# A planner's margin for VectorE and the first group with shared clusters, in a fused retention and MLP kernel

## The chip, the cores and the metric

The kernel runs on one core of one Trainium2 chip. The metric is the device time of one execution in microseconds (us); the time before is the median of 3 runs.

## The reference

For 8 batches and 8 heads, 576 positions of 64 elements, retention is computed: scores of q and k, scaled by 1/8, times a lower triangular decay of each head, times v. The result, laid out as 4608 tokens of 512 elements, goes through two dense layers with a squared ReLU between them.

```python
scores = scale * np.matmul(q, k.transpose(0, 1, 3, 2))
gamma = 1.0 - 2.0 ** (-5.0 - np.arange(H, dtype=np.float32))
Dmat = np.where(rel >= 0, gamma[:, None, None] ** rel[None, :, :], 0.0)
attn_out = np.matmul(scores * Dmat[None, :, :, :], v)
x = attn_out.transpose(0, 2, 1, 3).reshape(B * S, H * D)
h = x @ w_in                      # 512 -> 2048
r = np.maximum(h, 0.0)
return ((r * r) @ w_out)          # 2048 -> 512
```

## The kernel before

**Units and groups.** The tokens are cut into 36 units of 128 tokens: four full ones per batch, and one "tail" for each pair of batches. Two units make a group; there are 18 groups, 0 to 17, and the program works through them in order.

**Retention.** It is done in chunks with a running state. In each unit, TensorE makes scores (tile `psc`), sums of k and v for the state (`psS`), and outputs (`psO`), all as matmuls on 64x64 quarters of the array, issued by the helper `quad` (L343). VectorE masks the scores (`rT`, or `rx` in groups 0 to 3), updates the states (`stmp`, `Rm`, `R`) and multiplies the outputs by the decay into `xT`. Groups 0 to 3 come from paired loads (`pair`), with transposes on TensorE (`psT`); later units are loaded with `k`, `q`, `v`, cast on GpSimd (`kq`, `v`) and transposed by DMA (`kqT`).

**Clusters.** From group 4 on the matmuls of retention are issued in clusters. A group on its own has two: `fa` (scores and sums) and `fb` (outputs that read older states, a drain of TensorE, and the other outputs). From group `JOIN` on two neighbours share: `f1` is the first outputs of group g with the scores of g + 1, `f2` the sums of g + 1 with the remaining outputs of g. `add_ret` builds them.

**The dense layers.** `add_ff` cuts the 2048 hidden elements into 16 blocks of 128. A block of the first layer is 4 matmuls into a PSUM tile `ph` (L827; two blocks share one tile), followed by a ReLU on ScalarE (`rl`, L835) and a square on ScalarE or VectorE (`gT`). In groups 0 and 1 the second layer is 16 matmuls per unit into `po` (L865). From group 2 on it is a Strassen scheme of seven products (L916) that read `gT`, sums `gS` made by VectorE (L893), and differences `wT` of the weights. PSUM has four tiles for `ph`, `po` and their like.

**The weights** come in eight pieces of 1 MB, here called w0 to w3 (`wi`, of w_in, four hidden blocks each) and w4 to w7 (`wo`, of w_out). GpSimd and ScalarE each cast one half of a piece to 16 bit (L322). Loads, transposes and stores are issued by SyncE in one queue; a load waits for a free staging buffer. Until there is other work TensorE runs filler matmuls (`warm`, L247), 40 of them.

**What sets the order.** Only the first loads are listed by hand. Each piece of work is added to a `Schedule` with an engine, a priority key, a planned duration, what it depends on and which buffers it takes. `emit` plays the plan through once, when the program is built: whenever an engine is free it takes the ready item of lowest key. The instructions are then written out for each engine in the order in which they started in that plan. The chip follows this order whatever the real durations are; semaphores only make it wait. A result becomes ready for a user on another engine `LAT` microseconds after the end of its producer in the plan; buffers are released after the same time:

```python
push(now + (0.0 if w["eng"] == t["eng"] else t["lat"]), "dep", w)
```

Of the kernel before, what the change touches and what calls it, by code (L numbers as in the profile page):

```python
# [14 lines left out]

class Schedule:

    LAT = {"PE": 0.25, "ACT": 0.12, "DVE": 0.12, "POOL": 0.12, "SP": 2.1}

    def __init__(self, count):  # L20
        self.count = dict(count)
# [2 lines left out]
    def add(self, eng, key, dur, fn, deps=(), acq=(), after=None, lag=0.0):  # L24
        t = dict(eng=eng, key=key, dur=dur, fn=fn, acq=acq, n=len(self.tasks), users=[], free=[], lag=lag,
                 left=len(deps), ready=0.0, lat=self.LAT[eng] if after is None else after)
        for d in deps:
# [14 lines left out]
    def emit(self):  # L42
        ready = {e: [] for e in self.LAT}
        busy = {e: False for e in self.LAT}
        events = []
# [58 lines left out]
def kernel(  # L104
# [122 lines left out]
    SQ_ACT = (0, 1, 2, 3, 4, 5, 6)  # L227
    SPREAD = 0.1
    SQ_LATE = (1, 4, 6)
    JOIN = 7  # L230
    LAG = {"v2": 1.2, "w1": 1.3, "k4": 0.7, "q4": 0.5}
    LAG_T, LAG_O = 1.5, 5.0
    PAIRED = 8
# [115 lines left out]
    def add_unit(u, base):  # L349

        kind, b, c = units[u]
        tail = [tail_dec] if kind == "tail" else []

        def sorted_cast(op, out_, in_):
            op(out=out_.rearrange("p (n b a d) -> p n b a d", n=2, b=2, a=2),  # L355
               in_=in_.rearrange("p (n a b) d -> p n b a d", n=2, a=2))

        def fk():
            t = tile_of["kq", u] = cast.tile([P, 2, H * D], FP16, name="kq16", tag="kq16")
            sorted_cast(nc.gpsimd.tensor_copy, t[:, 0], tile_of["k32", u])  # L360

        def fq():
            sorted_cast(nc.gpsimd.tensor_copy, tile_of["kq", u][:, 1], tile_of["q32", u])

        def fv():
            t = tile_of["v16", u] = cast.tile([P, H, D], FP16, name="v16", tag="v16")
            nc.gpsimd.tensor_tensor(  # L367
                out=t, in0=tile_of["v32", u],
                in1=vdec[kind].rearrange("p (h o) -> p h o", o=1).to_broadcast([P, H, D]), op=ALU.mult)
        ck = add("POOL", base, 0.65, fk, deps=[loaded["k", u]], acq=("kq",))  # L370
        cq = add("POOL", base + 1, 0.62, fq, deps=[loaded["q", u], ck])
        cv = add("POOL", base + 2, 1.1, fv, deps=[loaded["v", u]] + tail, acq=("v16",))
        for what, t in (("k", ck), ("v", cv)):
            for w in gate.get((what, u), []):
                sched.need(w, t)
        T["casts", u] = [ck, cq, cv]
        sched.free("ld", [ck, cq, cv])
        def fx2():
            t = tile_of["kqT", u] = work.tile([P, 2 * NP, P], FP16, name="kqT", tag="kqT", bufs=6)
            nc.sync.dma_start_transpose(out=t, in_=tile_of["kq", u].rearrange("p x n -> p (x n)"))  # L380
        T["kqT", u] = [add("SP", -1, 2.7, fx2, deps=[ck, cq], acq=("kqT",), after=3.0, lag=LAG_T)]
# [162 lines left out]
    def units_of(g):  # L544
        return sorted(groups[g])
# [4 lines left out]
    def base_of(g):  # L550
        return (units_of(g)[0] - len(groups[g])) * L - EARLY
# [74 lines left out]
    def joined(g):  # L626

        return JOIN <= g < last_g

# [82 lines left out]
    def add_casts(g):  # L712
        for u in units_of(g):
            if u < PAIRED:
                if u % 2 == 0:
                    add_unit_pair(u, base_of(g) - 5)
                continue
            add_unit(u, base_of(g) - L * (2 if g > JOIN else 1) + 4 * (u - units_of(g)[0]))

# [336 lines left out]
```

## Time and profile before

| what | value |
| --- | --- |
| median of 3 runs | 292.76 us (292.64 to 292.85) |
| the profiled execution | 292.64 us |
| its span, first to last instruction | 290.9 us |
| TensorE busy | 283.0 us, 97% of the span |
| VectorE busy | 195.0 us, 67% |
| ScalarE busy | 187.5 us, 64% |
| GpSimd busy | 88.9 us, 31% |
| HBM, mean over the span | 159 GB/s |

Engines are named in the profile as PE (TensorE matmul), PEld (its weight load), DVE (VectorE), ACT (ScalarE), POOL (GpSimd) and SP (SyncE); a q behind the name is its sequencer. A line of the timeline has start and length in us, engine, line of the kernel, operation, output tile and inputs, shapes and count; brackets hold the idle time of the engine before it and what ended that. A line of the waits has the waiting instruction, what it waited for, us in total, times and the longest. A busy TensorE is not a TensorE at its peak, and the ends of its matmuls are modelled, so starts are compared.

### The profile page before, as it was taken

Reading aid. Unit: us, or ns where it says so; the run is one execution under the profiler, and the core shown is the slowest. Engines: PE = TensorE matmul, PEld = TensorE weight load, DVE = VectorE, ACT = ScalarE, POOL = GpSimd, SP = SyncE. Lnnn points to the kernel's source line nnn. Section 1 sums busy time; section 2 is a strip of 40 time slices with the busy share of each in tenths; the row PEclk is TensorE's granted clock in tenths of the full one; section 3 lists DMA queues with packets and bytes.
Section 4 is the critical chain, followed back from the end, with each engine's and each line's share of the span. In section 5 each row is a group of like instructions: output and inputs, shape, how many; then the busy total and the mean of one; then the engine's idle time right before and its main releaser. Section 6 shows DMA issues by size and latency. Waiting matters only on the chain.

```text
span 290.9 us, 10062 instructions
## 1 busy us (share of the span) xinstructions
PE 283.0 (97%) x4328; PEld 234.0 (80%) x4328; DVE 195.0 (67%) x430; ACT 187.5 (64%) x354; POOL 88.9 (31%) x123
## 2 busy tenths in 40 slices
PE   7989999999999999999999999999999999999994
PEld 2557765688888888888888888888888888888883
DVE  3796589748485848656868857667786865565632
ACT  6456966296757575867666666766767676747830
POOL 5343454524434234251616041615151400000000
PEclk9999999999999999999999999999999999999999
DMA  7999999999999899997998599979896820201004
GB/s 201 327 368 387 370 276 250 239 220 186 233 214 214 185 148 247 221 186 189 196 208 180 126 192 211 202 183 180 211 188 171 159 74 2 74 3 72 2 2 144
DMA packets 139421, 54.13 MB, mean 186 GB/s; under 512 B 118129, under 2 KB 130929, under 8 KB 139377
## 3 DMA queue, kind: packets, MB, share of 16 engines
q1 hardware_dynamic: 139072, 53.23, 81.9%
q8 instruction: 34, 0.56, 0.9%
q10 hardware_dynamic: 304, 0.26, 0.3%
q14 instruction: 11, 0.08, 0.1%
HBM read 36.70 MB, written 9.44 MB: 159 GB/s over the span
## 4 chain that ended last, share of the span: by engine, by line
PE 89%; DMA 6%; SPq 1%; issue 1%; POOL 1%; DVE 0%; DVEq 0%; POOLq 0%
PE ph L827 42%; PE po L916 34%; PE po L865 5%; PE psO L343 4%; DMA wi<-in_moe_w_in_dram 3%; DMA pair<-in_q_dram 3%; PE psc L343 2%; PE psS L343 2%; SPq L298 1%; POOL w_in L322 1%; PE psT L418 1%; DVE o L939 0%; POOL qx L403 0%; DVE p L968 0%; DVEq L939 0%
## 5 line engine op out<-in xcount | busy, mean ns | idle before, releaser
L827 PE MATMUL ph<-xT,w_in 128*128 128x256 f16 x1152 | 139.4, 273 | 0.2 <-POOL w_in L322 0.2
L827 PEld LDWEIGHTS <-w_in 128*128 128x128 f16 x1152 | 111.1, 98 | 14.8 <-POOL w_in L322 0.4
L835 ACT ACTIVATE rl<-ph 128x512 f16<-128x512 f32 x144 | 84.3, 589 | 46.9 <-PE ph L827 45.0
L845 ACT ACTIVATE gT<-rl 128x512 f16<-128x512 f16 x104 | 65.6, 631 | 3.0
L916 PEld LDWEIGHTS <-gS 128*128 128x128 f16 x512 | 49.4, 98 | 6.1 <-DVE gS L893 0.2
L916 PE MATMUL po<-wT,gS 128*128 128x256 f16 x384 | 52.4, 273 | 0.0
L893 DVE TENSOR_TENSOR gS<-gT,gS 128x512 f16<-128x512 f16 x64 | 35.1, 554 | 11.6 <-ACT gT L845 11.0
L916 PEld LDWEIGHTS <-gT 128*128 128x128 f16 x384 | 37.2, 98 | 4.4
L893 DVE TENSOR_TENSOR gS<-gT 128x512 f16<-128x512 f16 x64 | 30.7, 481 | 12.9 <-ACT gT L845 12.9
L916 PE MATMUL po<-w_out,gT 128*128 128x256 f16 x256 | 34.5, 273 | 0.0
L355 POOL CAST kq<-q 128x512 f16<-128x512 f32 x28 | 18.8, 673 | 45.7 <-DMA q<-in_q_dram 45.5
L367 POOL TENSOR_TENSOR v<-v,vdec_full 128x512 f16<-128x512 f32 x24 | 26.2, 1093 | 19.6 <-DMA v<-in_v_dram 14.4
L355 POOL CAST kq<-k 128x512 f16<-128x512 f32 x28 | 18.6, 666 | 44.4 <-DMA k<-in_k_dram 41.7
L847 DVE TENSOR_TENSOR gT<-rl 128x512 f16<-128x512 f16 x40 | 18.9, 473 | 14.7 <-ACT rl L835 14.2
L929 ACT COPY u<-po 128x256 f32<-128x256 f32 x32 | 11.8, 369 | 20.4 <-PE po L916 20.4
L939 DVE TENSOR_TENSOR o<-po,u 128x256 f32<-128x256 f32 x31 | 13.0, 421 | 16.2 <-PE po L916 8.3
L704 DVE TENSOR_TENSOR xT<-psO,gam_full 128x512 f16<-128x512 f32 x28 | 18.9, 686 | 7.5 <-PE psO L343 7.4
L643 DVE TENSOR_TENSOR rT<-psc,mask 128x512 f16<-128x512 f32 x28 | 18.3, 683 | 5.5 <-PE psc L343 5.2
L916 PE MATMUL po<-w_out,gS 128*128 128x256 f16 x128 | 17.0, 273 | 0.0
L916 PE MATMUL po<-wT,gT 128*128 128x256 f16 x128 | 16.8, 273 | 0.0
L939 DVE TENSOR_TENSOR o<-po,p 128x256 f32<-128x256 f32 x17 | 7.2, 424 | 13.7 <-ACT u L929 7.1
L865 PE MATMUL po<-w_out,gT 128*128 128x512 f16 x64 | 15.8, 380 | 0.0
(81 smaller groups left out, 244.1 us busy)
## 6 DMA issues: line engine op xcount, KB each, us to landing
out_dram<-o SPq DMA_DIRECT2D x31, 256.0 KB, 3.0
k<-in_k_dram SPq DMA_DIRECT2D x24, 256.0 KB, 4.5
q<-in_q_dram SPq DMA_DIRECT2D x24, 256.0 KB, 4.8
v<-in_v_dram SPq DMA_DIRECT2D x24, 256.0 KB, 5.3
wi<-in_moe_w_in_dram SPq DMA_DIRECT2D x4, 1024.0 KB, 10.1
wo<-in_moe_w_out_dram SPq DMA_DIRECT2D x4, 1024.0 KB, 9.7
pair<-in_k_dram SPq DMA_DIRECT2D x4, 512.0 KB, 7.0
pair<-in_q_dram SPq DMA_DIRECT2D x4, 512.0 KB, 7.0
```

The source lines that it names most:

```text
L343: nc.tensor.matmul(out_, lhsT=lhsT, rhs=rhs, start=start, stop=True, skip_group_check=True, tile_position=(64 * row, 64 * col))
L355: op(out=out_.rearrange("p (n b a d) -> p n b a d", n=2, b=2, a=2), in_=in_.rearrange("p (n a b) d -> p n b a d", n=2, a=2))
L367: nc.gpsimd.tensor_tensor(out=t, in0=tile_of["v32", u], in1=vdec[kind].rearrange("p (h o) -> p h o", o=1).to_broadcast([P, H, D]), op=ALU. ...
L704: nc.vector.tensor_tensor(out=tile_of["x", g][:, :, s * P:(s + 1) * P].rearrange("p n (c i) -> p c n i", c=2), in0=tile_of["psO", g][:, :, ...
L827: nc.tensor.matmul(tile_of["ph", g, fb][:, j, :], lhsT=w_in16[:, m, fi * P:(fi + 1) * P], rhs=tile_of["x", g][:, m, :], start=(m == 0), st ...
L835: nc.scalar.activation(out=t, in_=tile_of["ph", g, fb], func=ACTF.Relu)
L845: nc.scalar.activation(out=t, in_=rl, func=ACTF.Square)
L847: nc.vector.tensor_tensor(out=t, in0=rl, in1=rl, op=ALU.mult)
L865: nc.tensor.matmul(tile_of["po", u], lhsT=tile_of["g", g][:, fi, s * P:(s + 1) * P], rhs=w_out16[:, fi, :], start=(fi == 0), stop=(fi == N ...
L893: nc.vector.tensor_tensor(out=Sx(k, h), in0=in0(h), in1=in1(h), op=op)
L916: nc.tensor.matmul(tile_of["pb", g, bank], lhsT=left(i), rhs=right[:, i, :], start=(start and i == 0), stop=(i == HF - 1), skip_group_chec ...
L939: nc.vector.tensor_tensor(out=o_tile(u)[:, half * HM:(half + 1) * HM], in0=bank(x), in1=tile_of[name, g], op=ALU.add)
```

## The change

Two constants differ. The time that the plan lets pass until a result of VectorE counts as there on another engine goes from 0.12 to 0.3 us, and the first group with shared clusters from 7 to 8.

```diff
-    LAT = {"PE": 0.25, "ACT": 0.12, "DVE": 0.12, "POOL": 0.12, "SP": 2.1}
+    LAT = {"PE": 0.25, "ACT": 0.12, "DVE": 0.3, "POOL": 0.12, "SP": 2.1}
...
-    JOIN = 7
+    JOIN = 8
```

`JOIN` is read in two places: in `joined`, which tells whether a group shares, and in `add_casts`, where the casts of groups behind it get an earlier key.

```python
return JOIN <= g < last_g
...
add_unit(u, base_of(g) - L * (2 if g > JOIN else 1) + 4 * (u - units_of(g)[0]))
```

The instructions are the same in number and kind; what differs is their order. The order of GpSimd is unchanged. On TensorE, VectorE, ScalarE and SyncE items trade places throughout. On TensorE, group 7's `f1` and `f2` become its `fb` and group 8's `fa`. At the start of TensorE's order these lines move (a block is one first-layer block of the group named):

```diff
 group 0, blocks 1 to 4
-fillers, psO of group 1
 group 0, block 5
+psO of group 1
 group 0, blocks 6 to 12
-group 1, block 1
 group 0, blocks 13 to 16
-group 1, blocks 2 to 4
+group 1, block 1
 group 0, po 1 to 4 of the first unit
...
 group 0, po 13 to 16 of the first unit, all of the second unit
+group 1, blocks 15 and 16
 group 1, po
```

On ScalarE the casts of w3 to w7 each move ahead of one ReLU. On VectorE, at the start, the cast of v for the first pair moves ahead of a copy of `kqT`.

## The prediction

> **What bounds the kernel now.** I read the page first: busy shares, then the chain that ended last.
>
> ```profile
> PE 283.0 (97%) x4328; PEld 234.0 (80%) x4328; DVE 195.0 (67%) x430; ACT 187.5 (64%) x354; POOL 88.9 (31%) x123
> ...
> PEclk9999999999999999999999999999999999999999
> ...
> PE 89%; DMA 6%; SPq 1%; issue 1%; POOL 1%; DVE 0%; DVEq 0%; POOLq 0%
> ```
>
> TensorE has work for 97% of the span at full granted clock, and the chain is TensorE nearly throughout; VectorE, whose planning figure is changed, has a third of its time free. A busy share can hide waits, so next the waits of TensorE:
>
> ```profile
> PE warm L247 <- DVE junk L163: 1.3, 1, 1.3
> PE psO L343 <- DVE R L489: 0.9, 1, 0.9
> PE psT L418 <- DVE qx L403: 0.4, 1, 0.4
> PE psS L343 <- DVE vx L399: 0.3, 1, 0.3
> PE ph L827 <- POOL w_in L322: 0.2, 1, 0.2
> ```
>
> That is all. So I laid out the timeline of TensorE and of GpSimd around those waits:
>
> ```profile
> 20.02 1.04 PE L247 MATMUL warm<-junk 128*128 128x512 f16 x4
> 22.00 0.31 PE L343 MATMUL psO<-kqT,R 64*64 64x128 f16 x8 [0.94 <-DVE R L489]
> ...
> 23.09 4.10 PE L827 MATMUL ph<-xT,w_in 128*128 128x256 f16 x36
> 27.35 0.83 PE L827 MATMUL ph<-xT,w_in 128*128 128x256 f16 x6 [0.15 <-POOL w_in L322]
> ```
>
> ```profile
> 26.25 1.04 POOL L322 CAST w_in<-wi 128x1024 f16<-128x1024 f32 x1 [1.66 <-DMA wi<-in_moe_w_in_dram]
> 28.95 1.04 POOL L322 CAST w_out<-wo 128x1024 f16<-128x1024 f32 x1 [1.66 <-DMA wo<-in_moe_w_out_dram]
> 31.65 1.15 POOL L322 CAST w_out<-wo 128x1024 f16<-128x1024 f32 x1 [1.66 <-DMA wo<-in_moe_w_out_dram]
> 34.32 1.04 POOL L322 CAST w_out<-wo 128x1024 f16<-128x1024 f32 x1 [1.52 <-DMA wo<-in_moe_w_out_dram]
> 37.10 1.29 POOL L322 CAST w_out<-wo 128x1024 f16<-128x1024 f32 x1 [1.74 <-DMA wo<-in_moe_w_out_dram]
> ```
>
> Two regimes. Up to 38.45 the eight 1 MB weight pieces (w0 to w3 of w_in, w4 to w7 of w_out) are cast as they land, every 2.7 us, and TensorE can only fill the time between with what needs no later piece. After 38.45 TensorE never waits as much as 0.1 us: comparing starts of successive matmuls, I find only about 0.09 at each step into a cluster of 64x64 matmuls and 0.05 once near 228. What the start leaves undone at 38.45, and what TensorE's work costs after it, therefore sets the end one for one.
>
> Prices: a first-layer block (4 matmuls of ph) starts 0.437 after the last (16 in 33.89 to 35.63 = 1.74); a second-layer matmul of groups 0 and 1 (po, L865) 0.216.
>
> **Part 1, VectorE's margin 0.12 to 0.3: the start.** The planner holds work that reads VectorE's results back by 0.18, and the orders of TensorE, VectorE, ScalarE and SyncE shift; GpSimd's does not. I walk TensorE's new order.
>
> Before w1 (cast ends 20.63 + 1.04 = 21.67) the changes cost nothing: group 0's chain runs some 0.5 later on VectorE and the fillers (warm) stand elsewhere, but all of it still ends before w1, which the next block needs. If that cover went, the 0.5 would show, but then the next pin, w3, is still ahead.
>
> At w1: before, TensorE waits for R until 22.00, runs psO of group 1 (1.09), then blocks. After, block 5 of group 0 goes first (about 21.7 to 22.2), then psO to 23.3, then blocks 6 to 12: 7 x 0.437 = 3.06, to 26.4 (block 9 may add 0.1 for w2). Block 13 needs w3: 26.25 + 1.04, start 27.35 as before. In the old order block 1 of group 1 stood ahead of it (the ninth of the 36 matmuls at 23.09); in the new one it stands behind. TensorE idles some 0.95 where it idled 0.3.
>
> From 27.35: blocks 13 to 16 and one of group 1, 5 x 0.437 = 2.18, to 29.53. Then the first po, which needs w4: 28.95 + 1.04 + 0.06 (the lag of w3's cast to its matmul) = 30.05, idle 0.5. In the old order three more blocks stood there and nothing idled. Then 4 po 0.86, 6 blocks 2.62 (33.53, w5 at 32.8 is there), 4 po, 3 blocks 1.31 (35.71, w6 at 35.36 is there), 4 po, 4 blocks 1.75: 38.32. The next po needs w7, 37.10 + 1.29 + 0.06 = 38.45, where it starts in the old run too:
>
> ```profile
> 36.50 1.91 PE L827 MATMUL ph<-xT,w_in 128*128 128x256 f16 x16
> 38.45 1.89 PE L865 MATMUL po<-w_out,gT 128*128 128x512 f16 x8
> ```
>
> So both orders stand at the same po at 38.45, but the old one has all 16 blocks of group 1 behind it, the new one 14; blocks 15 and 16 come later, after group 0's last po. Left over: 2 x 0.437 = **+0.87**.
>
> ScalarE's casts of w3 to w7 move ahead of a Relu each. They start on arrival as before (26.22, 28.92, 31.62); the Relu queued behind slips about 1 us, so PSUM tiles and gT come later. With four ph/po tiles the tile needed at block 15 (28.2) is free at 27.9, the others have over 0.5. Cost 0, and 0.1 to 0.3 if a Relu is slower.
>
> Stores move behind loads and transposes on SyncE's queue. The transposes of group 4 land at 57.03 and 61.02 for a use at 64.73, later ones with 6 us or more to spare: 0. Moves of gS sums, o additions and state updates on VectorE: I compared, for each TensorE instruction, TensorE work between its producer and itself in both orders. It shrinks noticeably for two: the products of group 11 that read gS (3.93 to 3.49 us, slack in the trace 0.40) and the second cluster of group 8 after its masks (2.27 to 2.05, slack 0.87). It grows by 0.15 and 0.43 where slack was least, groups 13 (0.06) and 12 (0.20). Gain 0.05, cost 0 to 0.1: taken as 0. Bounds for everything in the steady part: -0.05 to +0.6, the upper end if the queue ahead of such a step is longer by one VectorE operation (0.55) that meets no slack.
>
> **Part 2, JOIN 7 to 8.** Group 7's two shared clusters (L343: out1 of 7 with scores of 8, then sums of 8 with out2 of 7) become an own output cluster of 7 with a drain in it, and an own scores and sums cluster of 8. Prices, from start to the start of the next instruction, by rows of the same matmul counts:
>
> ```profile
> 86.74 0.21 PE L343 MATMUL psO<-kqT,Rm 64*64 64x64 f16 x1
> ...
> 86.87 0.19 PE L343 MATMUL psO<-kqT,R 64*64 64x64 f16 x1
> 87.16 0.32 PE L343 MATMUL psO<-rT,v 64*64 64x64 f16 x16
> ...
> 87.67 0.50 PE L916 MATMUL po<-wT,gT 128*128 128x256 f16 x3
> ```
>
> An own output cluster of 64 matmuls takes 86.74 to 87.67 = 0.93, with 0.29 of standstill at the drain (86.87 to 87.16). Own scores and sums, 48 matmuls, take 0.51 (group 4, 64.73 to 65.24). Replaced: 117.34 to 117.85 = 0.51 and 120.14 to 120.78 = 0.64. So 0.93 + 0.51 - 0.51 - 0.64 = **+0.28**. x of group 7 comes 3 us sooner, which nobody waits for.
>
> Steps into 64x64 mode: 69.61 + 8 x 0.109 = 70.48, but the cluster starts at 70.58, so about 0.1 each. Both orders have 39 such steps: 0.
> The Trainium skill ("TensorEngine Tiling (Array Packing)", Key Properties) says that changing the tiling mode drains TensorE. By that rule alone un-sharing costs only as far as it adds mode changes, and it adds none, so by it the sum would be +0.87; the rows show that the drain written inside the cluster is what costs.
>
> **Sum.** Profiled execution 292.64 (span 290.9 and 1.7 around it). +0.87 + 0.28 = +1.15, to 293.79. It lies 0.12 under the median of the runs, so the median becomes **293.9**. The last 4 us after TensorE's end keep their order.
>
> **Rivals.**
> A, new waits in the steady part on top (to +1.75, about 294.5): the reordered VectorE queue meets a TensorE step without slack. For it: slack of 0.06 to 0.4 at the gS products of groups 11 to 13. Against: most distances grow. 0.15.
> B, not slower: weights land sooner. SyncE's issue of w1 waits 1.0 us for VectorE's vx of v0 (SPq L308 <- DVE vx L399), and the new order puts vx ahead of a kqT copy, so w1 could be issued up to 1.0 earlier. Where w3 and w4 come d sooner, the two idle times shrink by d, and from d = 0.6 on the change is inside the noise; at d = 1.0 the time is +0.15, about 292.9. For: the order. Against: v0 lands only at 8.69 and vx began at 9.12, so 0.43 is all there is (+0.72, about 293.5), and the pieces land 2.7 apart, back to back, which says bandwidth and not issue sets them. 0.12 for an end within the noise.
> C, the margin helps and start pays nothing: faster only if TensorE's idle up to 38.45 shrank by 0.6 more than the drain costs; I see no row for it. 0.04.
> The forecast itself, slower by 0.7 to 1.4: 0.69.
>
> **How the numbers follow.** 0.2% (0.59 us) is about what a measurement of this kernel can tell from no change. Faster by more: C, 0.04. Within: B, 0.12. Slower: forecast and A, 0.84. Range: low 293.3 (B's 0.43 with 0.2 of luck), high 294.6 (A).
>
> **What would show it.** Right: a wait of TensorE for w_in of about 0.9 before 27.35 and one for w_out of about 0.5 before 30.05; po at 38.45 with 8 ph matmuls still to come near 43.7; the cluster of group 7 taking 0.93 with a gap of 0.29; waits after 40 below 0.2 in sum. Wrong: the w7 cast ending before 38.0 (B), or TensorE waits on VectorE or ScalarE after 60 us (A).

## The result and the profile after

The changed kernel takes 294.33 us (median of 4 runs, 294.20 to 294.34) beside 292.81 us of the kernel before on the same chip (292.64 to 292.98): slower, ratio 1.0051, interval 1.0034 to 1.0068. The profiled executions are 294.34 and 292.64 us, with spans of 292.5 and 290.9 us at full granted clock.

The page after: busy shares and the chain that ended last.

```profile
PE 283.0 (97%) x4328; PEld 234.0 (80%) x4328; DVE 195.1 (67%) x430; ACT 187.2 (64%) x354; POOL 91.2 (31%) x123
...
PEclk9999999999999999999999999999999999999999
...
PE 88%; DMA 6%; SPq 3%; POOL 1%; issue 0%; DVE 0%; DVEq 0%; POOLq 0%
```

TensorE is as busy as before to the tenth of a us; only GpSimd is 2.3 us busier, with the same 123 instructions. Nothing here says where 1.7 us went. The waits of TensorE say more (waiting instruction, what it waited for, us in total, times, longest):

```profile
PE ph L827 <- POOL w_in L322: 2.1, 2, 1.4
PE warm L247 <- DVE junk L163: 1.3, 1, 1.3
PE psS L343 <- POOL vx L399: 1.0, 1, 1.0
PE po L865 <- POOL w_out L322: 0.4, 1, 0.4
```

The waits for R and for qx are gone; in their place TensorE waits longer for casts of weights (POOL w_in, w_out). All are ahead of 40 us. TensorE's timeline of that stretch:

```profile
21.83 0.61 PE L827 MATMUL ph<-xT,w_in 128*128 128x256 f16 x4 [1.41 <-POOL w_in L322]
22.37 0.31 PE L343 MATMUL psO<-kqT,R 64*64 64x128 f16 x8
...
23.46 3.25 PE L827 MATMUL ph<-xT,w_in 128*128 128x256 f16 x28
27.43 2.36 PE L827 MATMUL ph<-xT,w_in 128*128 128x256 f16 x20 [0.72 <-POOL w_in L322]
30.22 1.02 PE L865 MATMUL po<-w_out,gT 128*128 128x512 f16 x4 [0.44 <-POOL w_out L322]
...
36.74 1.91 PE L827 MATMUL ph<-xT,w_in 128*128 128x256 f16 x16
38.69 0.59 PE L865 MATMUL po<-w_out,gT 128*128 128x512 f16 x2
```

Seven blocks (28 matmuls) run after psO, then TensorE stands until w3's cast; five blocks run and it stands until w4's. By starts, 7 x 0.437 from 23.46 ends at 26.52, so the first standstill is 0.91; the second, after 27.43 + 5 x 0.437 = 29.62, is 0.60. The 13th po starts at 38.69, not 38.45. Further on in the same timeline:

```profile
43.46 0.59 PE L865 MATMUL po<-w_out,gT 128*128 128x512 f16 x2
43.89 1.04 PE L827 MATMUL ph<-xT,w_in 128*128 128x256 f16 x8
44.77 0.59 PE L865 MATMUL po<-w_out,gT 128*128 128x512 f16 x2
```

Eight ph matmuls, the two blocks left over, take 43.89 to 44.77, 0.87 before rounding. The kernel before has none here. TensorE's last pair of matmuls starts at 288.35 instead of 286.72 (six matmuls, 0.65, into the last rows of eight, which start at 287.70 and 286.06): **+1.63**, which splits at landmarks that both traces have:

| stretch of TensorE | before | after | difference |
| --- | --- | --- | --- |
| start of group 0's 13th po | 38.45 | 38.69 | +0.24 |
| from there to group 4's first scores | 26.28 | 27.39 | +1.11, of it 0.87 the two blocks |
| from there to the last pair of matmuls | 221.99 | 222.27 | +0.28 |

### The profile page after: what moved, and what is told of

It reads as the page before. It is cut to its first block, busy times and chain, and to the rows that moved or that the text cites. A ratio compares the mean times of both kernels' runs of the same rounds, so it can differ in the third digit from the quotient of the medians.

```text
span 292.5 us, 10068 instructions
## 1 busy us (share of the span) xinstructions
PE 283.0 (97%) x4328; PEld 234.0 (80%) x4328; DVE 195.1 (67%) x430; ACT 187.2 (64%) x354; POOL 91.2 (31%) x123
## 4 chain that ended last, share of the span: by engine, by line
PE 88%; DMA 6%; SPq 3%; POOL 1%; issue 0%; DVE 0%; DVEq 0%; POOLq 0%
PE ph L827 41%; PE po L916 34%; PE po L865 5%; PE psO L343 4%; DMA wo<-in_moe_w_out_dram 3%; DMA pair<-in_v_dram 3%; SPq L298 2%; PE psc L343 2%; PE psS L343 2%; PE psT L418 1%; SPq L308 1%; POOL vx L399 1%; POOL w_out L322 0%; DVE o L939 0%; DVE p L968 0%
## 5 line engine op out<-in xcount | busy, mean ns | idle before, releaser
L893 DVE TENSOR_TENSOR gS<-gT,gS 128x512 f16<-128x512 f16 x64 | 35.9, 563 | 15.2 <-ACT gT L845 14.6
L893 DVE TENSOR_TENSOR gS<-gT 128x512 f16<-128x512 f16 x64 | 32.0, 501 | 12.6 <-ACT gT L845 12.6
L367 POOL TENSOR_TENSOR v<-v,vdec_full 128x512 f16<-128x512 f32 x24 | 26.8, 1118 | 18.7 <-DMA v<-in_v_dram 15.5
L847 DVE TENSOR_TENSOR gT<-rl 128x512 f16<-128x512 f16 x40 | 18.2, 456 | 16.3 <-ACT rl L835 15.7
```

Of the source, the lines that this page charges most:

```text
L367: nc.gpsimd.tensor_tensor(out=t, in0=tile_of["v32", u], in1=vdec[kind].rearrange("p (h o) -> p h o", o=1).to_broadcast([P, H, D]), op=ALU. ...
L893: nc.vector.tensor_tensor(out=Sx(k, h), in0=in0(h), in1=in1(h), op=op)
```

## The experiments

Theory T of the expectations has the prediction's two terms, the two blocks left undone at the 13th po (0.87) and the drain that JOIN 8 brings back (0.28), and two that were read off the trace after: a later cast of w7 (0.24), and one more cluster (0.24). TensorE's landmarks of the table help where the timed difference is near the noise. They are from one execution each, and the landing of the weights moves the first of them from execution to execution, as the section on the 13th po shows.

### The two parts, each alone

```diff
-    JOIN = 7
+    JOIN = 8
```

> JOIN 8 with VectorE's margin left at 0.12. Its order has no group 1 block left over at group 0's 13th po and 33 steps into clusters after it, as the old order has; only group 7's two clusters differ. Theory T (the cost is paid in four places: two blocks left over 0.87, a later w7 cast 0.24, one more cluster and a parted pair of clusters 0.24, the drain in group 7's own output cluster 0.28): +0.28 us, about 293.05, with the first po after w7 at 38.4 to 38.5 as before. Rival S (the looser plan and the unshared group lose a little everywhere): a share of 1.6, with waits of TensorE spread over the span.

Measured: 293.17 us, ratio 1.0011 (1.0003 to 1.0020). The 13th po is at 38.62, later than the expected 38.4 to 38.5. From it to TensorE's last pair are 248.55 us, before 248.27: +0.28. Group 7's cluster takes 0.92. The drain is sized right.

```diff
-    LAT = {"PE": 0.25, "ACT": 0.12, "DVE": 0.12, "POOL": 0.12, "SP": 2.1}
+    LAT = {"PE": 0.25, "ACT": 0.12, "DVE": 0.3, "POOL": 0.12, "SP": 2.1}
```

> VectorE's margin 0.3 with JOIN left at 7. Its order has two blocks of group 1 left over and 34 steps into clusters after group 0's 13th po. Theory T: +1.35 us (0.87 + 0.24 + 0.24), about 294.1; the first scores of group 4 start some 1.35 later than before and the end keeps that distance. Rival S: less than 1.35 by group 4 and more after it.

Measured: 293.89 us, ratio 1.0035 (1.0023 to 1.0047). Po at 38.56, the two blocks at 43.76, group 4's first scores at 65.94, after that 221.97 us as before (221.99). So the margin costs 1.2 at TensorE's end, all of it ahead of group 4. T had 1.35; it missed at the 13th po, which is 0.11 later than before and not 0.24. The timed parts add up within their intervals: 0.35% and 0.11% beside 0.51%.

### The margin in one half of the plan

Inside the planner, the margin is switched by the plan's own time; the second kernel has the two values exchanged.

```diff
+                    lat = (0.3 if now >= 40.0 else 0.12) if t["eng"] == "DVE" else t["lat"]
...
-                        push(now + (0.0 if w["eng"] == t["eng"] else t["lat"]), "dep", w)
+                        push(now + (0.0 if w["eng"] == t["eng"] else lat), "dep", w)
...
-                        push(now + t["lat"], "free", g)
+                        push(now + lat, "free", g)
```

> Margin 0.12 in the plan's first 40 us and 0.3 after it, JOIN 7. No block is left over and 33 steps into clusters follow, but the order after 40 us has the wider margin. Theory T: within 0.1 us of before (the 0.05 wait near 228 gone), about 292.75. Rival S: slower by a good part of 1.35. Rival M (the margin does help where it is meant to): faster by 0.2 or more.

> Margin 0.3 in the plan's first 40 us and 0.12 after it, JOIN 7. Two blocks are left over, 34 steps into clusters follow. Theory T: +1.1 to +1.35 us, 293.9 to 294.1, all of it there when group 4's first scores start. Rival S: near 0.

Measured: with the margin only after 40 us, 292.67 us, ratio 0.9994 (0.9986 to 1.0003); with it only before 40 us, 294.20 us, ratio 1.0048 (1.0036 to 1.0060), 0.1 over the expected 293.9 to 294.1. TensorE's timeline where the blocks would lie, of the first (line numbers are one higher in these two kernels):

```profile
42.55 0.61 PE L419 MATMUL psT<-ident,qx 128*128 128x128 f16 x8
42.99 1.89 PE L866 MATMUL po<-w_out,gT 128*128 128x512 f16 x8
```

and of the second:

```profile
43.38 0.59 PE L866 MATMUL po<-w_out,gT 128*128 128x512 f16 x2
43.81 1.04 PE L828 MATMUL ph<-xT,w_in 128*128 128x256 f16 x8
44.69 0.59 PE L866 MATMUL po<-w_out,gT 128*128 128x512 f16 x2
```

Nothing is left over in the first; the second has both blocks at 43.81, and group 4's first scores at 66.00, 1.27 later than before. In the steady part, where the prediction's rival A saw its danger, the margin does nothing that the timed runs can tell, for better or worse. In the trace of the first kernel TensorE needs 222.17 us from group 4's first scores to its last pair, 0.18 more than before; the kernel with the margin throughout and JOIN 7 needs 221.97.

### Real landing times in the plan

The plan puts w3's cast at 25.05; on the chip it starts at 26.25. Theory L: with the weights where the traces have them, the planner fills the waiting times with the blocks again, with either margin.

```diff
-    LAG = {"v2": 1.2, "w1": 1.3, "k4": 0.7, "q4": 0.5}
+    LAG = {"v2": 1.2, "w1": 1.3, "w2": 1.3, "w3": 1.2, "w4": 1.15, "w5": 1.1, "w6": 1.05, "w7": 1.05, "k4": 0.7, "q4": 0.5}
```

> The kernel before, with the plan's landing times of w2 to w7 set some 1.1 us later, to where the trace has them (LAG of w2 1.3, w3 1.2, w4 1.15, w5 1.1, w6 and w7 1.05). Its order puts two to three more blocks of group 1 ahead of w3 and none is left over at group 0's 13th po; 35 steps into clusters follow instead of 33. Theory T: TensorE's idle before w3 (0.3) goes, the po after w7 starts at most 0.25 sooner, the two steps cost 0.2: within 0.3 of before.

The next kernel has this and the margin of 0.3, with JOIN 7.

> As the run before it, with VectorE's margin 0.3 (JOIN 7). Theory L (the margin costs because the plan has the weights too early: with a later x of group 1 it believes that no block of group 1 is ready when w3 comes, though on the chip there is time for it): no block is left over, TensorE's idle before w3 and w4 goes, within 0.3 us of before, where the margin alone cost 1.1 to 1.35. Rival S (the margin itself costs, wherever the weights land): 1.1 to 1.35 slower again.

Measured: 294.07 and 293.82 us, ratios 1.0043 (1.0030 to 1.0056) and 1.0043 (1.0029 to 1.0056). Both miss the expected time, which was within 0.3 of before. On the blocks L was right: with the margin and real landings none is left over, po is at 38.58. The second kernel's +1.16 is what rival S expected, but not by S's way, for the blocks are not there. The time went elsewhere. TensorE's timeline of the kernel with the landings alone:

```profile
36.24 1.04 PE L827 MATMUL ph<-xT,w_in 128*128 128x256 f16 x8
38.28 2.10 PE L865 MATMUL po<-w_out,gT 128*128 128x512 f16 x9 [1.01 <-POOL w_out L322]
...
42.19 0.81 PE L865 MATMUL po<-w_out,gT 128*128 128x512 f16 x3
43.94 0.45 PE L343 MATMUL psS<-vx,kx 64*64 64x64 f16 x32 [0.93 <-POOL vx L399]
```

TensorE is through all blocks of group 1 early and waits 1.01 for w7. That wait by itself costs nothing: the 13th po starts at 38.28, before at 38.45, with the same matmuls behind it. The loss comes after it. TensorE needs 28.22 us from the 13th po to group 4, before 26.28. Of these 1.94 us, 0.93 is the wait at the sums of the next pair, whose v GpSimd scales at 42.34 to 43.88 as in the kernel before (42.33); the plan, played through, has that scaling at 41.48. TensorE also steps into seven clusters instead of five (0.1 each), and the clusters take 4.65 instead of 3.93, a wait of 0.28 at 53.96 among it. With the margin as well it is 27.50: again seven clusters, which take 4.49, and a wait of 0.38 for v. So a truer plan for six loads of weights left the next thing that the plan has too early, and a new order of clusters that cost time of its own.

### Sharing from earlier groups

JOIN 8 costs 0.28, so JOIN 4, 5 and 6 might each gain that per group. JOIN 4 first:

> The kernel before with JOIN 4: groups 4 to 6 share clusters too, so three own output clusters with their drains go, and the loads of groups 5 to 7 are cast sooner. Theory T (0.28 a group): -0.85 us, about 291.9, TensorE without waits after 60 us. Rival W (casts and transposes of the early groups come too late for shared clusters): TensorE waits on kqT at group 4 to 6, no gain or a loss.

Measured: 294.09 us, ratio 1.0041 (1.0027 to 1.0055). From the 13th po to the last pair 249.63 us, 1.36 more than before instead of 0.85 less. TensorE waits 0.34 for rT at 79.67, 0.46 for u at 83.26, and 0.44 at 134.13 for nothing that the profile shows; none of these is for kqT, as rival W had it. The other two steps came later, each with the old margin and with 0.3 from 40 us of the plan on:

> JOIN from 7 to 6, the margin at 0.12: the opposite step to the change's second part. Group 6 shares its clusters too, so one drain inside a cluster goes. Theory T (each shared group is worth the 0.28 us measured between JOIN 7 and 8): TensorE's last matmul group 0.28 earlier counted from the 13th po, time 292.4 where the kernel before gives 292.7 in the same call. Rival W (sharing earlier makes TensorE meet VectorE's masks and ScalarE's copy of u, as with JOIN 4): one or more waits of 0.2 us and over between 70 and 125 us at the shared clusters of group 6, and no gain or a loss up to 1.0.

> JOIN 6, and VectorE's margin 0.12 while the plan's time is below 40 us and 0.3 after. Theory T: the margin in the steady part takes away such waits on VectorE as JOIN 6 alone shows (sum of the waits after 40 us below 0.1), so 292.4, the same as or faster than JOIN 6 with 0.12. Rival N (the margin in the plan does not move where the chip waits): the same waits within 0.1 as JOIN 6 with 0.12, and the same time within 0.3.

> JOIN 5, the margin at 0.12. Theory T: two drains fewer than with JOIN 7, 0.57 us less from the 13th po to TensorE's end, time 292.1 where the kernel before gives 292.7. Rival W: waits at the masks and the copies of u of group 5 or 6 (with JOIN 4 they were 0.34, 0.46 and 0.28 at 79 to 85 us), time 292.7 to 293.7.

> JOIN 5, and VectorE's margin 0.12 while the plan's time is below 40 us and 0.3 after. Theory T: waits on VectorE after 40 us below those of JOIN 5 with 0.12, time 292.1 to 292.4. Rival N: the same waits within 0.1 and the same time within 0.3 as JOIN 5 with 0.12.

Measured: JOIN 6, 293.91 us with the old margin (1.0039; 1.0024 to 1.0054) and 293.78 with 0.3 (1.0034; 1.0022 to 1.0047). JOIN 5, 293.83 (1.0037; 1.0023 to 1.0052) and 293.68 (1.0027; 1.0016 to 1.0038). None gains. Each has a wait at the first group that shares, for x and not for the masks or u that rival W named; here TensorE and then VectorE with JOIN 6 and the old margin:

```profile
106.96 0.45 PE L343 MATMUL psS<-v,kq 64*64 64x64 f16 x32
...
108.61 1.47 PE L916 MATMUL po<-wT,gS 128*128 128x256 f16 x12
111.06 2.14 PE L827 MATMUL ph<-xT,w_in 128*128 128x256 f16 x18 [0.97 <-DVE xT L704]
```

```profile
106.95 1.27 DVE L893 TENSOR_TENSOR gS<-gT 128x512 f16<-128x512 f16 x1
...
108.47 0.68 DVE L704 TENSOR_TENSOR xT<-psO,gam_full 128x512 f16<-128x512 f32 x1
109.07 0.41 DVE L664 TENSOR_TENSOR Rm<-psS,R 128x256 f16<-128x256 f32 x1
109.52 0.42 DVE L668 TENSOR_TENSOR stmp<-psS,Rm 128x256 f32<-128x256 f32 x1
109.97 0.42 DVE L672 TENSOR_TENSOR R<-stmp,dec 128x256 f16<-128x256 f32 x1
110.32 0.68 DVE L704 TENSOR_TENSOR xT<-psO,gam_full 128x512 f16<-128x512 f32 x1
```

Group 6's second cluster starts at 106.96 and its first block wants x at 110.09, 3.13 later. But VectorE makes the second xT only after a state update, until 111.00. In the kernel before, group 7 is the first to share: 4.15 us lie between its f2 (120.14) and its first block (124.29), and the second xT ends at 123.53, 0.76 ahead. From the start of f2 to the end of the second xT are 3.39 us there and 4.04 here: before it, a sum gS takes 1.27 here beside GpSimd's scaling of v (106.61 to 107.93), where its like takes 0.42. With 3.39 the wait would still be 0.26, an estimate from these rows. With JOIN 5 the first block wants x about 2.5 after the start of f2. JOIN 7 is thus the earliest of those tried whose first shared group has the distance.

The margin hardly moves the wait with JOIN 6 (0.97 and 0.99), so rival N holds there. With JOIN 5 it goes from 1.51 to 1.10, and N holds for the time alone. These waits are the largest part of the loss. A rest of 0.3 to 0.7 us per kernel (lengths from the 13th po to the last pair, with 0.28 taken off for each drain and the waits put in; with JOIN 4 some 0.9) I have not split, and the 0.44 without a releaser stays open.

An own output cluster without its drain wasn't tried.

### The late 13th po

TensorE's 13th po waits for w7's cast, which takes 1.49 instead of 1.29. GpSimd and VectorE of the changed kernel:

```profile
37.15 1.49 POOL L322 CAST w_out<-wo 128x1024 f16<-128x1024 f32 x1 [1.55 <-DVE gT L847]
```

```profile
37.05 0.68 DVE L778 TENSOR_TENSOR wT<-w_out 128x1024 f16<-128x1024 f16 x1
```

In the kernel before, wT starts at 36.80 and ends 0.39 into the cast; here it ends 0.58 into it. In both the cast ends 0.90 after wT.

But a later cast is not what makes the po late. By starts, TensorE's own work brings it to the po at 36.74 + 16 x 0.109 = 38.48, so it stands 0.20 for the cast. In the kernel before it arrives at 36.50 + 1.74 = 38.24 and stands 0.20 as well. wT comes behind a gT of TensorE's own blocks and starts 1.44 and 1.43 ahead of these arrivals, so the end of w7's cast moves with TensorE. What differs is where TensorE last stood before: in the old order it works without a stop from w3's cast on, in the new one from w4's, with one block more between the first and the 13th po. In the eight kernels that keep the old order at the start (before, JOIN 8 alone, the margin after 40 us, and all with JOIN 4 to 6), the 13th po comes 12.19 to 12.20 after w3's cast starts. In the three with the new order and wT in its place (after, the margin alone, the margin before 40 us) it comes 9.65 to 9.67 after w4's cast starts, and 12.36 after w3's. So the new order costs 0.16 up to here. The other 0.08 of the 0.24 is w3's cast itself, at 26.33 instead of 26.25; among the eight equal orders it starts anywhere from 25.95 to 26.43.

The experiment gives the first and third wT a planned delay of 2 us in the changed kernel, so that w7's cast finds VectorE free of it.

```diff
-            ts.append(add("DVE", 3 * L + i, 0.85, f, deps=sum((wcast[j] for j in range(4, 8)), [])))
+            ts.append(add("DVE", 3 * L + i, 0.85, f, deps=sum((wcast[j] for j in range(4, 8)), []), lag=2.0 if i in (0, 2) else 0.0))
```

> The changed kernel with the first weight differences of VectorE (wT) planned 2 us later, behind w7's cast; TensorE's order is the same up to the last third of group 1. Theory T (the w7 cast on GpSimd took 1.49 because wT ran at the same time; 1.04 alone): cast 1.04 to 1.1, the po behind it without a wait of 0.2, 0.15 to 0.25 faster than the changed kernel, about 294.1. Rival P (the cast's length has nothing to do with VectorE): cast near 1.5 again, no gain.

Measured: 293.97 us, ratio to the kernel before 1.0046 (1.0033 to 1.0059), against the changed kernel's 1.0051: not told apart. GpSimd's line:

```profile
37.04 1.15 POOL L322 CAST w_out<-wo 128x1024 f16<-128x1024 f32 x1 [1.69 <-DMA wo<-in_moe_w_out_dram]
```

The cast is 0.34 shorter; the 0.11 over 1.04 goes with a gT that still ran 0.25 into it. But TensorE starts the 13th po at 38.64 all the same, now without a wait: its first po stood at 30.38 (30.22 in the changed kernel), and its own work from there takes 8.26. By the same work the changed kernel reached the po at 30.22 + 8.26 = 38.48 and stood the 0.2 to 38.69 for the cast. That wT stretches the cast, and that TensorE's standstill goes with it, is shown; that this shortens the kernel is not, because this run lost 0.16 ahead of it, at half clock (last section). Four of the six timed runs have a granted clock of 1.000; their median is 293.84, 1.18 over the kernel before measured beside them, where the change has 1.52. That points to the expected gain, but these four were picked after the result.

## Why the prediction was right

The forecast was 293.9 in a range of 293.3 to 294.6; measured 294.33. The two main mechanisms were right, the sum 0.5 short. That the result still lies inside the range is partly luck: its upper end was held by rival A's waits in the steady part, which did not come. What came instead were two terms that the prediction had put at nothing.

- **Two blocks left, +0.87**: right in size, place (43.89) and cause. The standstills it rests on were forecast at 0.95 and 0.5 and were 0.91 and 0.60. The margin before 40 us alone brings it, the margin after 40 us alone does not.
- **JOIN 8, +0.28**: right (the prediction's four rows add up to 0.29). Group 7's cluster took 0.93 with the drain in it, from the first row here to the second, and the table's last row, as well as JOIN 8 alone, gives 0.28:

```profile
117.82 0.21 PE L343 MATMUL psO<-kqT,Rm 64*64 64x64 f16 x1
...
118.75 0.39 PE L916 MATMUL po<-wT,gT 128*128 128x256 f16 x2
```

- **"Both orders stand at the same po at 38.45"**: this step failed by 0.24. It took the end of w7's cast from the trace of before and held it fixed as a pin behind TensorE's arrival at 38.32. But the cast's end moves with TensorE, which stood 0.20 for it in both kernels, and the arrival was 38.48: w4's cast, the real pin of the new order, began 0.08 later in that execution and took 1.14 instead of 1.04, with a gT under way when it started. The order's own share is 0.16. In every run the 13th po starts 0.05 after w7's cast or later.
- **"Steps into 64x64 mode: 39 in both, 0"**: mis-sized. The totals are equal, but one step fewer lies in the start, where TensorE has time over, and one more after 38.45, at the price that the prediction gave, 0.1. There outputs of group 2 and scores of the next pair, before in one cluster, stand apart:

```profile
49.49 0.30 PE L343 MATMUL psO<-kqT,R 64*64 64x128 f16 x4
...
50.56 0.60 PE L865 MATMUL po<-w_out,gT 128*128 128x512 f16 x2
51.09 0.42 PE L343 MATMUL psc<-kqT 64*64 64x128 f16 x16
```

By starts, all clusters from the 13th po to group 4 take 4.06 instead of 3.93 us; with the step, 0.23 of the 0.24 that the two blocks leave open in the table's second row.
- **Waits in the steady part** (rival A): none over 0.1 after 40 us, so groups 8 and 11, whose distances shrank, wait for nothing either.
- **Rival B**: w7's load landed at 37.09, in the kernel before at 37.05. The early cast of v did not bring the weights forward in this execution.
- **Sum**: 0.24 + 0.87 + 0.24 + 0.28 = 1.63 at TensorE's last pair; the profiled executions differ by 1.70, the medians by 1.52. With 0.16 for the order alone in place of the first 0.24 the sum is 1.55.

## What to carry to other kernels

When a planner's order is changed, look up which pinned event (here each weight's cast) ends each stretch, and count what is still to do behind the last pin: work that fits ahead of it is free, work behind it is paid in full. Counts such as steps or waits are compared behind that pin, not over the whole kernel. A duration beside which a moved instruction runs is not a constant of the trace: ask what ran next to it. An event that looks like a pin can follow the very engine that waits for it, as w7's cast did here through gT and wT; compare its distance from the arrivals in several traces before holding it fixed. And a plan that is truer in one place was not faster here, because the next late arrival was still wrong in it; measure it.

## What the runs showed of the hardware

**GpSimd's cast and VectorE.** A cast of 128x1024 takes 1.04 us alone. Where a VectorE operation with two inputs in SBUF (wT, gT) is under way when it starts, it grows by the overlap less 0.13 to 0.15: 0.24 of overlap gives 1.14, 0.39 gives 1.29, 0.46 gives 1.36, 0.58 gives 1.49; 0.11 gives nothing. In other words the cast ends 0.90 after that operation. A VectorE operation with one input in PSUM leaves it at 1.04: in the kernel before, stmp with 0.26 of overlap (w1) and xT with 0.42 (w2). Where the cast starts first it stays at 1.04 and VectorE's gT takes 1.21 instead of 0.43 (29.06 in the kernel before, beside w4's cast). The Trainium skill ("SBUF — State Buffer", Who interferes with whom) says that such a VectorE instruction contends with GpSimd's reads and that the one that issues second blocks fully; the runs agree on who waits, but the cast that is held up ends 0.14 sooner than a full 1.04 after the VectorE operation.

**Clock.** The run with wT later shows half the granted clock for some 3.4 us after TensorE had idled 1.54 us (20.35 to 21.89). Rows of windows: from and to, length, busy us of PE, PEld, DVE, ACT and POOL, then the granted clock, DMA share and GB/s:

```profile
22.00:23.00 1.00, 0.90 (x24) 0.52 (x26) 0.86 (x3) 0.00 (x0) 0.00 (x0) 0.98 1.04 375
23.00:24.00 1.00, 1.00 (x41) 0.83 (x34) 0.44 (x2) 0.52 (x1) 0.49 (x1) 0.50 1.04 383
...
26.00:27.00 1.00, 1.00 (x10) 0.81 (x9) 0.10 (x1) 0.81 (x1) 0.78 (x1) 0.81 1.07 381
```

Blocks took 0.79 to 0.85 there; most of it was taken from the standstills for w3 and w4, the rest is the 0.16 by which that run's first po is late. The kernel with the margin before 40 us idled 1.89 at the same place and kept full clock in its trace. It is not the kernel that decides, though. Such a stretch of 3.41 us at half clock brings the mean of a span of 292 us down to 0.994. Two of the six timed runs with wT later have that mean, two of the five with the margin before 40 us, and one of the six with margin and real landings (idle 1.89 in its trace). All other runs with a clock on record have 0.997 or more, and in the traces of those kernels TensorE idles at most 1.46 there. So the drop came only with the three longest of these idle times, and only in some executions. The Trainium skill ("TensorE: Matmul & The Clock Gate", Part 1) has the drop follow an idle window of about 3.4 us; this run idled less than half of that, and what decides between executions is open.
